# Batch 0 of an attention-and-experts kernel: normalising after the values product, and low key parts made by GpSimd

## The chip, the cores and the metric

The kernel runs on one core of a Trainium2 chip. The metric is device time in microseconds (us) of one execution. The profile is one profiled execution of the same program; its times are us from the start of its span unless marked ns.

## The reference

Attention over 4 batches of 8 heads, 576 positions, 64 columns a head, with a mask in blocks of 64; its output goes through two feed-forward stages.

```python
scores = scale * np.matmul(q, k.transpose(0, 1, 3, 2))
scores = np.where(block_i >= block_j, scores, -1000000000.0)
attn = np.exp(scores - np.max(scores, axis=-1, keepdims=True))
attn = attn / (np.sum(attn, axis=-1, keepdims=True) + 1e-09)
x = np.matmul(attn, v)                      # -> (2304, 512) over batches and heads
h = np.maximum(np.maximum(x @ w1, x @ w2), x @ w3)
x = h @ w_out                               # first feed-forward stage, d_ff 768
for e in range(4):                          # second stage, 4 experts, d_ff 1024
    out += p[:, e:e + 1] * (np.maximum(x @ w1[e], 0.0) @ w2[e])
```

All of it is float32. The division by the sum of a row is the normalising that the change moves.

## The kernel before

The program has three parts in time: the attention of batch 0, with nothing of the first feed-forward stage to fill TensorE; the attention of batches 1 to 3, between whose steps the first feed-forward stage (`moe1`, line 505) of the batch before is laid; and the second feed-forward stage, which takes the rest of the span.

Heads go in pairs (pairs 0 to 3 are batch 0). `prep_pair` makes of a pair's raw keys and queries a rounded high part and a low part that is the rest: of the keys, ScalarE rounds (line 85; of pair 0 VectorE, line 87) and VectorE subtracts on 64 partitions (line 122); of the queries, ScalarE rounds (133) and VectorE makes the rest (135). For pair 0 this goes head by head, for the others both heads in one instruction. `scores` multiplies them (190, and 195 for the mask), VectorE takes the row minimum of the negated scores (208), ScalarE takes the exponential with the row sum beside it (215). A head has four tiles of probabilities, 128, 384, 512 and 256 columns wide; a fifth, `p4`, 576 wide, holds the last 64 rows of both heads of a pair and is made with the second.

`normalise`, which is put in `later` and called one step after the scores, adds 1e-9 to the sums (223), takes their reciprocals (224), and GpSimd multiplies each tile of probabilities by its reciprocals in place (226). `turn_probs` then transposes the probabilities on TensorE (264) into PSUM, and ScalarE and VectorE copy them out to `eh` (273 and 289). Batch 0's `values32` multiplies them by the values (310, 318, 322) and ScalarE copies the result to `xf` (327 to 334). `xf` has the channels of both heads on its 128 partitions and the 576 positions along its columns. `moe1_inputs` splits `xf` into a high and a low part (523 and 524) for the feed-forward stage. Probabilities, transposes and scores share four PSUM banks (`ps_x`, tag `x`); `eh` has one buffer.

Beside this, from the first microseconds on, the class `Convert` turns 26 pieces of feed-forward weights from the 64-bit form in which they come into high and low parts: for each piece two instructions on ScalarE and one more to round (429, 431, 85), two on GpSimd (436, 443) and three on VectorE (438, 439, 452). They are needed by `moe1` of batch 0.

The order of each engine's instructions is not the order of the program text: a planner simulates the engines with a cost model of its own and orders each engine's instructions by what it takes to be ready first, so an edit in one place can change the order in others. Each engine then works through its list in order. Batch 0's pairs are `g < 4` in `prep_pair`, its heads `g < H` (8) elsewhere.

Of the kernel before, what the change touches and what calls it, by code (L numbers as in the profile page):

```python
# [6 lines left out]
F32 = mybir.dt.float32  # L7
# [5 lines left out]
ALU = mybir.AluOpType  # L13
# [5 lines left out]
P = 128  # L19
# [5 lines left out]
def program(tc, q, k, v, w123, w_out, probs, e_w1, e_w2, out):  # L25
    nc = tc.nc

    B, H, D, S = q.shape[0], 2 * q.shape[1], q.shape[2] // 2, q.shape[4]
# [12 lines left out]
    def f(ap):  # L41
        return ap.bitcast(F32)
# [3 lines left out]
    ident = const.tile([P, P], F32, name="ident")  # L46
# [10 lines left out]
    arena = big.tile([P, KD * NT], F32, name="arena")  # L57
# [8 lines left out]
    ps_x = attn.enter_context(tc.tile_pool(name="ps_x", bufs=4, space=PSUM, side="right"))  # L66
# [12 lines left out]
    lo, hi, both = slice(0, 64), slice(64, 128), slice(0, P)  # L79
# [25 lines left out]
    def prep_pair(g):  # L105


        raw, vraw = pairs[g]["raw"], pairs[g]["vraw"]
        if g < NPAIR and g % 2:

            spare = mp.tile([P, 2 * QW + 2 * S], F32R, name="spare", tag="hh")
            q1, q2 = spare[:, 0:QW], spare[:, QW:2 * QW]
            kk = spare[:, 2 * QW:].rearrange("x (h s) -> x h s", h=2)
        else:
            q1, q2 = (ap_.tile([P, QW], F32R, name=x, tag=x, bufs=1)[:] for x in ("q1", "q2"))
            kk = ap_.tile([P, 2, S], F32R, name="kk", tag="kk", bufs=1)[:]
        for x in (q1, q2):
            nc.gpsimd.memset(x[:, QT + 64:QT + 128].bitcast(U32), 0)

        def keys(hs):  # L120
            (rounded if g else lambda _, to, x: rounded(nc.vector, to, x))(nc.scalar, kk[:, hs], raw[:, 1, hs])
            nc.vector.tensor_tensor(kk[hi, hs], raw[hi, 1, hs], f(kk[hi, hs]), op=ALU.subtract)

        def queries(hs):
            x = raw[:, 0, hs]
            parts = []
            for to in (q1, q2):
                main = to[:, 0:QT].rearrange("x (h s) -> x h s", h=2)[:, hs]
                tail = to[:, QT:QW].rearrange("x (t s) -> x t s", s=64)[:, 0:3:2][:, hs]
                parts.append((main, tail))  # L130
            srcs = (x[:, :, 0:S - 64], x[:, :, S - 64:S])
            for high, src in zip(parts[0], srcs):
                nc.scalar.activation(high, src, ACTF.Copy, scale=-scale)  # L133
            for high, low, src in zip(*parts, srcs):
                nc.vector.scalar_tensor_tensor(low, src, -scale, f(high), op0=ALU.mult, op1=ALU.subtract)

        if g == 0:
            for h in range(2):
                keys(slice(h, h + 1))
                queries(slice(h, h + 1))  # L140
            yield
        else:
            keys(slice(0, 2))
            yield
            queries(slice(0, 2))
        pairs[g].update(q1=q1, q2=q2, kk=kk)
        if g < NPAIR:
            return
        vs = ap_.tile([P, 2, 5, P], F32R, name="vs", tag="vs", bufs=2)
        vh = vs[:, :, :, 0:64]  # L150
        src = vraw.rearrange("p j h d -> p h j d")
        rounded(nc.gpsimd, vh, src)
        nc.gpsimd.tensor_tensor(vs[:, :, :, 64:128], src, f(vh), op=ALU.subtract)
        pairs[g]["vs"] = vs
# [8 lines left out]
    def scores(g, grp):  # L163
        pair, h = pairs[g // 2], g % 2
        if grp == 0:
            heads[g] = dict(
                p=[None] * 4,
                mn=ap_.tile([P, 5], F32, name="mn", tag="mn", bufs=3),
                sm=ap_.tile([P, 5, 2], F32, name="sm", tag="sm", bufs=3),
            )  # L170
        mn, sm, pt = heads[g]["mn"], heads[g]["sm"][:, :, 0], heads[g]["p"]
        masked = g < 2 * H
        c0 = 3 * grp
        sets = []
        for tag, cols, plan in GROUPS[1][h] if grp else GROUPS[0]:
            st = (ps_x if tag == "x" else ps_c).tile([P, cols], F32, name="st", tag=tag)
            sets.append((st, plan))
            for i, o, w in plan:

                if i == 4:  # L180
                    todo = [(QT + 64 * x, x) for x in range(2)]
                else:
                    todo = [(h * QT // 2 + P * i, h)]
                c = 0
                while c < w:
                    n = min(w - c, 512 - (o + c) % 512)
                    terms = [(part, q0, x) for q0, x in todo for part in ("q1", "q2")]
                    ends = masked and i < 4 and c + n == w
                    for m, (part, q0, x) in enumerate(terms):
                        nc.tensor.matmul(  # L190
                            out=st[:, o + c:o + c + n], lhsT=pair[part][:, q0:q0 + P],
                            rhs=pair["kk"][:, x, c:c + n], start=m == 0, stop=m == len(terms) - 1 and not ends,
                        )
                    if ends:
                        nc.tensor.matmul(
                            out=st[:, o + w - 64:o + w], lhsT=corner, rhs=corner[:, 0:64], start=False, stop=True
                        )
                    c += n
        c = c0
        done = []  # L200
        for st, plan in sets:
            for i, o, w in plan:
                if i < 4 and not masked:
                    nc.vector.memset(st[lo, o + w - 64:o + w], 1e30)
            mine = [(c + n, *x) for n, x in enumerate(plan)]
            c += len(plan)
            for col, i, o, w in mine:
                nc.vector.tensor_reduce(mn[:, col:col + 1], st[:, o:o + w], axis=AX.X, op=ALU.min)  # L208
            for col, i, o, w in mine:
                x = ap_.tile([P, w], F32, name=f"p{i}", tag=f"p{i}", bufs=2 if i == 4 else 3)  # L210
                if i == 4:
                    pair["p4"] = x
                else:
                    pt[i] = x
                nc.scalar.activation(  # L215
                    x, st[:, o:o + w], ACTF.Exp, bias=mn[:, col:col + 1], scale=-1.0,
                    accum_out=sm[:, col:col + 1],
                )
                done.append((col, x))

        def normalise():
            cs = slice(c0, c)
            nc.vector.tensor_scalar(sm[:, cs], sm[:, cs], 1e-9, None, op0=ALU.add)  # L223
            nc.vector.reciprocal(sm[:, cs], sm[:, cs])
            for col, x in done:
                nc.gpsimd.tensor_scalar(x, x, sm[:, col:col + 1], 1.0, op0=ALU.mult, op1=ALU.mult)  # L226

        later.append(normalise)


# [70 lines left out]
    def values32(g, part):  # L301


        pair, hd, h = pairs[g // 2], heads[g], g % 2
        eh, vraw = pair["eh"], pair["vraw"]
        own = lo if h == 0 else hi
        both_v = [vraw[:, j].rearrange("p h d -> p (h d)") for j in range(5)]
        if part == 0:
            hd["pv"] = [ps_v.tile([P, 512], F32, name=f"pv{i}", tag="v") for i in range(2)]
            nc.tensor.matmul(  # L310
                out=hd["pv"][0][:, 0:P], lhsT=both_v[0], rhs=eh[:, ZERO + 4 * h], start=True, stop=True
            )
        pv = hd["pv"][1]

        for j in ((0, 1), (2, 3))[part]:
            q0 = P * (max(1, j) - 1)
            n = 3 - q0 // P + h
            nc.tensor.matmul(
                out=pv[:, q0:q0 + n * P], lhsT=both_v[j], rhs=row(eh, j, h, n), start=j == 0, stop=h == 0 and j == 3
            )  # L320
        if part and h:
            nc.tensor.matmul(out=pv[:, 384:512], lhsT=both_v[4], rhs=eh[:, LAST], start=False, stop=True)
        if part == 0 and h == 0:
            pairs[g // 2]["xf"] = mp.tile([P, S], F32, name="xf", tag="xf", bufs=4)
        xf = pairs[g // 2]["xf"]
        if part == 0:
            nc.scalar.copy(xf[own, 0:P], hd["pv"][0][own, 0:P])
            return
        if h == 0:
            nc.scalar.copy(xf[lo, P:512], pv[lo, 0:384])  # L330
        else:
            nc.scalar.copy(xf[hi, P:512], pv[hi, 0:384])
            nc.scalar.copy(xf[lo, 512:S], pv[lo, 384:448])
            nc.scalar.copy(xf[hi, 512:S], pv[hi, 448:512])
        del heads[g]

    def values(g, part):
# [294 lines left out]
    rt = ExitStack()  # L632
# [576 lines left out]
    for e in range(E):  # L1209
        for g in range(NG):  # L1210
            begins, ends = e == 0 and g == 0, e == E - 1 and g == NG - 1
            wo = []
            hs = [[], []]
# [129 lines left out]
```

## Time and profile before

| | |
|---|---|
| median of 3 runs | 1255.24 us (1250.58, 1255.24, 2066.23) |
| the profiled execution's own time | 1249.91 us, of which span 1248.1 us |
| TensorE matmul busy | 1211.2 us, 97% of the span |
| VectorE (DVE) busy | 929.7 us, 74% |
| ScalarE (ACT) busy | 517.8 us, 41% |
| GpSimd (POOL) busy | 357.1 us, 29% |
| granted TensorE clock, mean of the span | 0.996 |

Busy shares are means over stages with different limits. The change touches batch 0 alone, so what it is worth has to be read from the first stretch of the span, and from how that stretch hands over to the next.

### The profile page before, as it was taken

Reading aid. Unit: us, or ns where it says so; the run is one execution under the profiler, and the core shown is the slowest. Engines: PE = TensorE matmul, PEld = TensorE weight load, DVE = VectorE, ACT = ScalarE, POOL = GpSimd, SP = SyncE. Lnnn points to the kernel's source line nnn. Section 1 sums busy time; section 2 is a strip of 40 time slices with the busy share of each in tenths; the row PEclk is TensorE's granted clock in tenths of the full one; section 3 lists DMA queues with packets and bytes.
Section 4 is the critical chain, followed back from the end, with each engine's and each line's share of the span. In section 5 each row is a group of like instructions: output and inputs, shape, how many; then the busy total and the mean of one; then the engine's idle time right before and its main releaser. Section 6 shows DMA issues by size and latency. Waiting matters only on the chain.

```text
span 1248.1 us, 19730 instructions
## 1 busy us (share of the span) xinstructions
PE 1211.2 (97%) x7417; PEld 1157.8 (93%) x7417; DVE 929.7 (74%) x1716; ACT 517.8 (41%) x1076; POOL 357.1 (29%) x444
## 2 busy tenths in 40 slices
PE   7879998999999999999999999999999999999998
PEld 5669997999999999989999998999999999999998
DVE  7978988666565634377888896758787888686896
ACT  7977767544544421233444441233232223322222
POOL 3957786454344212243333341000000000000000
PEclk9999999999999999999999999999999999999999
DMA  8745574554533488478887864778888887776754
GB/s 304 248 164 197 170 265 161 172 153 155 183 102 119 120 287 304 150 303 332 312 311 296 310 247 162 287 274 316 300 306 311 315 314 281 253 258 228 253 210 170
DMA packets 82644, 299.69 MB, mean 240 GB/s; under 512 B 8748, under 2 KB 18036, under 8 KB 69492
## 3 DMA queue, kind: packets, MB, share of 16 engines
q1 hardware_dynamic: 82548, 298.42, 67.3%
q8 instruction: 59, 0.97, 0.3%
q14 instruction: 37, 0.30, 0.1%
HBM read 215.26 MB, written 83.14 MB: 239 GB/s over the span
## 4 chain that ended last, share of the span: by engine, by line
PE 74%; DVE 10%; DMA 5%; POOL 4%; ACT 3%; issue 3%; SPq 0%; DVEq 0%; ACTq 0%; POOLq 0%
PE m L858 24%; PE m L505 19%; PE o L1017 17%; PE st L190 3%; PE pv L359 2%; PE o L940 2%; PE o L943 2%; PE o L944 2%; DMA t<-in_e_w 2%; PE m L1017 2%; POOL p L226 2%; PE tt L264 2%; DVE mn L208 2%; DMA part<-in_e_w 1%; POOL arena L443 1%
## 5 line engine op out<-in xcount | busy, mean ns | idle before, releaser
L505 PE MATMUL m<-xh,wt 128*128 128x288 f32 x1120 | 238.4, 298 | 0.7 <-ACT mt L541 0.4
L858 PE MATMUL m<-t,w 128*128 128x384 f32 x1152 | 228.5, 336 | 0.0
L1017 PE MATMUL o<-hx,w 128*128 128x384 f32 x1176 | 225.7, 337 | 0.0
L1017 PEld LDWEIGHTS o<-hx,w 128*128 128x128 f32 x1176 | 207.8, 188 | 0.1
L858 PEld LDWEIGHTS m<-t,w 128*128 128x128 f32 x1152 | 203.4, 188 | 2.5 <-DVE tmp L878 0.4
L505 PEld LDWEIGHTS m<-xh,wt 128*128 128x128 f32 x1120 | 183.7, 188 | 1.6 <-DVE mt L543 0.8
L858 PE MATMUL m<-b,w 128*128 128x384 f32 x864 | 175.7, 337 | 2.0 <-ACT tmp L883 2.0
L505 PE MATMUL m<-xl,wt 128*128 128x288 f32 x560 | 165.3, 295 | 0.0
L858 PEld LDWEIGHTS m<-b,w 128*128 128x128 f32 x864 | 153.2, 188 | 5.1 <-ACT tmp L883 2.3
L226 POOL TENSOR_SCALAR p<-p,sm 128x128 f32<-128x128 f32 (+1 forms) x144 | 98.7, 702 | 52.1 <-DVE sm L223 17.0
L505 PEld LDWEIGHTS m<-xl,wt 128*128 128x128 f32 x560 | 105.3, 188 | 0.3
L878 DVE TENSOR_TENSOR tmp<-m,tmp 128x384 f32<-128x384 f32 x144 | 77.9, 550 | 19.4 <-PE m L858 19.2
L505 PE MATMUL m<-hh,wo 128*128 128x288 f32 x384 | 81.3, 299 | 2.9 <-ACT arena L554 1.3
L215 ACT ACTIVATE p<-st,mn 128x128 f32<-128x128 f32 (+3 forms) x144 | 78.5, 555 | 8.2 <-DVE mn L208 6.3
L988 ACT CAST hx<-hq 128x768 fp32r<-128x768 f32 x49 | 40.6, 837 | 99.0 <-PE o L1017 75.9
L190 PE MATMUL st<-kk,q 128*128 128x128 f32 (+4 forms) x336 | 71.2, 340 | 8.7 <-ACT q L133 5.5
L940 PE MATMUL o<-w,hh 128*128 128x512 f32 x192 | 74.7, 391 | 0.9 <-ACT hh L918 0.6
L813 POOL TENSOR_TENSOR w<-part,w 128x512 fp32r<-128x512 f32 x32 | 49.2, 1557 | 91.3 <-ACT w L811 61.2
L943 PE MATMUL o<-w,hh 128*128 128x512 f32 x192 | 74.7, 390 | 0.0
L944 PE MATMUL o<-w,hl 128*128 128x512 f32 x192 | 74.1, 390 | 0.0
L543 DVE TENSOR_TENSOR mt<-m,mt 128x288 f32<-128x288 f32 x96 | 43.2, 452 | 40.3 <-PE m L505 39.9
L264 PE MATMUL tt<-ident,p 128*128 128x128 f32 x400 | 61.0, 278 | 9.8 <-POOL p L226 5.4
(169 smaller groups left out, 2173.8 us busy)
## 6 DMA issues: line engine op xcount, KB each, us to landing
w<-kb SPq DMA_DIRECT2D x55, 1024.0 KB, 6.1
w<-ka SPq DMA_DIRECT2D x30, 1792.0 KB, 7.9
ka<-w SPq DMA_DIRECT2D x16, 1792.0 KB, 6.7
wt<-held SPq DMA_DIRECT2D x54, 512.0 KB, 4.1
kb<-part SPq DMA_DIRECT2D x16, 1024.0 KB, 7.0
kb<-w SPq DMA_DIRECT2D x16, 768.0 KB, 4.7
arena<-in_w SPq DMA_DIRECT2D x18, 512.0 KB, 4.0
wo<-held SPq DMA_DIRECT2D x12, 768.0 KB, 4.5
```

The source lines that it names most:

```text
L190: nc.tensor.matmul(out=st[:, o + c:o + c + n], lhsT=pair[part][:, q0:q0 + P], rhs=pair["kk"][:, x, c:c + n], start=m == 0, stop=m == len(t ...
L215: nc.scalar.activation(x, st[:, o:o + w], ACTF.Exp, bias=mn[:, col:col + 1], scale=-1.0, accum_out=sm[:, col:col + 1],)
L226: nc.gpsimd.tensor_scalar(x, x, sm[:, col:col + 1], 1.0, op0=ALU.mult, op1=ALU.mult)
L264: nc.tensor.transpose(tt[:, c:c + P], pt[i][:, k0:k0 + P], ident)
L505: nc.tensor.matmul(out=out_, lhsT=w, rhs=x, start=m == 0, stop=m == n - 1)
L813: eng.tensor_tensor(w[:, a:b, 1], raw[:, a:b], f(w[:, a:b, 0]), op=ALU.subtract)
L858: ins = nc.tensor.matmul(out=m, lhsT=a, rhs=b, start=start and n == 0, stop=stop and n == 3 * KH - 1, skip_group_check=True,)
L878: nc.vector.tensor_tensor(t, x, y, op=ALU.add)
L940: ins = nc.tensor.matmul(out=o, lhsT=hh[:, ts], rhs=wh, start=i == 0, stop=False)
L943: nc.tensor.matmul(out=o, lhsT=hh[:, ts], rhs=wl, start=False, stop=False)
L944: nc.tensor.matmul(out=o, lhsT=hl[:, ts], rhs=wh, start=False, stop=i == G - 1)
L1017: nc.tensor.matmul(out=o, lhsT=a, rhs=b, start=start and m == 0, stop=stop and m == 2, skip_group_check=True,)
```

## The change

In batch 0 the four tiles of a head's probabilities are no longer multiplied by the reciprocals of their row sums; the fifth tile, `p4`, still is. Instead GpSimd copies the reciprocals, each repeated over 64 columns, to `rb`, a place in an idle part of `arena` (two places, taken by turns of the pairs): per head one copy of three columns of reciprocals and one of a single column. After the pair's values product, TensorE transposes the four 128x128 blocks of `rb` into a PSUM tile `rt` of the four shared banks, which makes them a tile of reciprocals by channel and position, and VectorE multiplies the first 512 columns of `xf` by it. And for batch 0's pairs GpSimd takes over the subtraction that makes the low part of the keys, but for that of the very first head.

```diff
         def keys(hs):
-            nc.vector.tensor_tensor(kk[hi, hs], raw[hi, 1, hs], f(kk[hi, hs]), op=ALU.subtract)
+            (nc.gpsimd if g < 4 and hs != slice(0, 1) else nc.vector).tensor_tensor(
+                kk[hi, hs], raw[hi, 1, hs], f(kk[hi, hs]), op=ALU.subtract
+            )
...
             nc.vector.reciprocal(sm[:, cs], sm[:, cs])
+            if g < H:
+
+                if grp == 0 and h == 0:
+                    o = (2 + 4 * (g // 2 % 2)) * P
+                    pair["rb"] = arena[:, o:o + 4 * P].rearrange("p (i h c) -> p i h c", i=4, h=2)
+                rb = pair["rb"][:, 0:3, h] if grp == 0 else pair["rb"][:, 3:4, h]
+                rs = sm[:, c0:c] if grp == 0 else sm[:, c - 1:c]
+                nc.gpsimd.tensor_copy(rb, rs.unsqueeze(2).to_broadcast([P, c - c0 if grp == 0 else 1, 64]))
             for col, x in done:
+                if g < H and x is not pair.get("p4"):
+                    continue
                 nc.gpsimd.tensor_scalar(x, x, sm[:, col:col + 1], 1.0, op0=ALU.mult, op1=ALU.mult)
...
             nc.scalar.copy(xf[hi, 512:S], pv[hi, 448:512])
+
+            rt = ps_x.tile([P, 512], F32, name="rt", tag="x")
+            for n, i in enumerate((0, 2, 3, 1)):
+                nc.tensor.transpose(
+                    rt[:, P * i:P * (i + 1)], pair["rb"][:, n].rearrange("p h c -> p (h c)"), ident
+                )
+            nc.vector.tensor_tensor(xf[:, 0:512], rt, xf[:, 0:512], op=ALU.mult)
         del heads[g]
```

## Rows read from the trace of the kernel before

**Rows 1.** Busy us (and instructions) of each engine by stretch, granted clock, DMA share, GB/s.

```profile
10.00:20.00 10.00, 7.74 (x38) 6.60 (x36) 7.33 (x19) 9.72 (x24) 3.93 (x9) 0.86 1.03 414
...
30.00:40.00 10.00, 8.70 (x55) 6.80 (x53) 9.69 (x17) 9.90 (x26) 9.75 (x13) 1.00 0.79 263
40.00:50.00 10.00, 8.31 (x40) 6.06 (x39) 9.81 (x18) 9.13 (x25) 8.46 (x11) 0.83 0.54 186
...
60.00:70.00 10.00, 8.29 (x50) 6.32 (x51) 5.83 (x16) 7.76 (x20) 8.13 (x12) 1.00 0.51 174
...
100.00:120.00 20.00, 19.32 (x142) 18.15 (x142) 17.73 (x35) 13.02 (x29) 19.34 (x24) 1.00 0.58 187
```

**Rows 2.** The chain of work, 0 to 92 us: start, us, what.

```profile
by line: POOL p L226 11.9%; DVE mn L208 8.9%; issue 8.3%; PE pv L318 7.1%; POOL arena L443 6.7%; PE st L190 6.2%; ACT p L215 5.6%; DMA arena<-in_q 5.4%; DVE spare L122 4.0%; PE tt L264 3.3%; PE m L505 3.0%; DVE q L135 2.3%; DVE xl L524 2.2%
...
11.41 1.35 DVE spare L122
...
19.96 1.50 DVE kk L122
...
31.03 2.33 DVE spare L122
...
44.55 2.29 POOL p L226 x4
...
60.67 2.05 POOL p L226 x4
...
78.97 2.36 POOL p L226 x2
...
82.03 4.49 PE pv L318 x8
...
89.17 2.21 PE m L505 x16
```

**Rows 3.** GpSimd's groups by shape, 0 to 90 us: busy us, mean ns, idle before.

```profile
L226 POOL TENSOR_SCALAR p<-p,sm 128x384 f32<-128x384 f32 x10 | 7.7, 765 | 0.0
L226 POOL TENSOR_SCALAR p<-p,sm 128x512 f32<-128x512 f32 x10 | 7.4, 738 | 0.0
L226 POOL TENSOR_SCALAR p<-p,sm 128x256 f32<-128x256 f32 x10 | 7.2, 725 | 0.0
...
L226 POOL TENSOR_SCALAR p<-p,sm 128x128 f32<-128x128 f32 x10 | 4.3, 432 | 5.3 <-ACT p L215 2.0 <-ACT wo L85 1.9 <-DVE sm L224 0.9
```

**Rows 4.** Line 226 alone, 76 to 90 us: ns min/median/max, first and last start.

```profile
L226 POOL TENSOR_SCALAR p<-p,sm x9: 367/690/1651, 78.6 to 86.6; 128x128 f32<-128x128 f32 x2, 128x384 f32<-128x384 f32 x2, 128x512 f32<-128x512 f32 x2, 128x256 f32<-128x256 f32 x2
```

**Rows 5.** Who waited for whom, 0 to 92 us: us in total, times, longest.

```profile
PEld tt L264 <- POOL p L226: 7.3, 4, 4.6
...
PEld st L190 <- DVE eh L289: 1.9, 2, 1.5
```

**Rows 6.** Single lines over the whole span: ns min/median/max, first and last start.

```profile
L122 DVE TENSOR_TENSOR kk<-arena,kk x9: 755/1355/1885, 4.6 to 343.9; 64x1152 fp32r<-64x1152 f32 x7, 64x576 fp32r<-64x576 f32 x2
...
L122 DVE TENSOR_TENSOR spare<-raw,spare x2: 1355/1842/2329, 11.4 to 31.0; 64x1152 fp32r<-64x1152 f32 x2
...
L153 POOL TENSOR_TENSOR vs<-vraw,vs x12: 1553/1572/2034, 39.5 to 381.2; 128x640 fp32r<-128x640 f32 x12
...
L546 POOL TENSOR_TENSOR hl<-mt,hh x48: 793/807/1792, 110.0 to 501.8; 128x288 fp32r<-128x288 f32 x48
...
L118 POOL MEMSET q<- x28: 147/152/163, 1.0 to 369.1; 128x64 uint32 x28
```

**Rows 7.** VectorE's groups by shape, 0 to 90 us.

```profile
L292 DVE TENSOR_TENSOR eh<-tt,eh 128x512 fp32r<-128x512 f32 x2 | 1.3, 687 | 3.5 <-ACT eh L291 3.5
```

**Rows 8.** Instructions in order of time, TensorE 24 to 26 us, VectorE 14 to 17 us.

```profile
24.75 1.07 PE L264 MATMUL tt<-ident,p 128*128 128x128 f32 x8
...
15.99 0.27 DVE L135 SCALAR_TENSOR_TENSOR spare<-raw,spare 128x128 fp32r<-128x128 f32 x1
```

**Rows 9.** TensorE alone by stretch: busy us, granted clock, DMA share, GB/s.

```profile
82.00:84.00 2.00, 2.00 (x4) 0.50 0.47 177
```

## The prediction, made before the result was known

> **What bounds the kernel now.** I read the table of busy time by stretch first. There the reader is to see two regimes. From 100 us on TensorE is busy 19.32 of 20 us; in batch 0's stage, from 30 to 50 us, it is busy 8.3 to 8.7 of 10, while VectorE shows 9.69 and 9.81, ScalarE 9.90 and 9.13 and GpSimd 9.75 and 8.46 [rows 1]. So batch 0 is bound by three engines at once, none of them TensorE, and what follows by TensorE. Then the chain of work up to 92 us: batch 0 hands over at 89.17, where line 505 begins [rows 2]. A microsecond taken out ahead of that point can be worth a microsecond at the end, since what follows is mostly a full TensorE; after it, the change alters nothing but the planner's order.
>
> The chain shows which engine ends last and where. VectorE's low keys (line 122) stand in it with 1.35 us at 11.41, 1.50 at 19.96 and 2.33 at 31.03; GpSimd's normalising (226) with 11.9% of 92 us, 10.9 us [rows 2]. Both are what the change takes away, so the naive reading is a gain of 5.2 and 10.9 us. Two things cut it. The first is whose normalising it is: GpSimd has treated ten tiles of each shape by 90 us, so ten heads [rows 3], and the nine instructions that start between 78.6 and 86.6 us are those of the last two of them, heads 8 and 9, which are batch 1's and keep theirs [rows 4]. The piece of 2.36 us at 78.97 [rows 2] therefore stays, and with it the one wait of 4.6 us that is most of the 7.3 us that TensorE's transposes wait for line 226 [rows 5]. The second is what is late next, which is taken stretch by stretch below.
>
> **What it removes and adds, engine by engine.** *GpSimd*: a head's four tiles cost 0.432 + 0.765 + 0.738 + 0.725 = 2.66 us [rows 3], eight heads 21.3 us, gone. Added are three low keys of 1152 columns and one of 576. GpSimd has no such row; its two-input float32 rows are 1.572 us for 640 columns and 0.807 for 288 [rows 6], that is 2.17 ns a column and 0.18 us to start with, hence about 2.68 and 1.43 us, 9.5 us in all. By VectorE's own 1.355 as the lower end it is 4.7, by the slowest of the 640-column rows (2.034 us, 3.18 ns a column) 12.8; I take 9.5, as the two rows do the same operation. Added too are sixteen copies of repeated reciprocals. No row shows one: the 64-column clearing of 0.152 us [rows 6] is a lower end for each, the 384-column product at 0.765 [rows 3] an upper. I take 0.45 us for three columns and 0.25 for one, near the 128-column row (0.432), 5.6 us in all, between 2.4 and 12.2. GpSimd is so left 21.3 - 9.5 - 5.6 = 6.2 us less to do.
>
> *VectorE*: four instructions of line 122 go, 0.755 + 1.355 + 1.50 + 2.33 = 5.9 us [rows 2 and 6]. Added are four products of `rt` with `xf`, each of 128x512 with one input in PSUM, as the subtraction of line 292, 0.687 us [rows 7]: 2.7 us. Net 3.2 us less.
>
> *TensorE*: sixteen more transposes. Eight of them take 1.07 us at the full clock [rows 8], so 0.13 each and 2.1 us together. They lie in a stage in which TensorE is idle 1.3 to 2.3 of every 10 us [rows 1]; cost nothing while that cover lasts, 2.1 us without it. *ScalarE* loses and gains no instruction.
>
> **The new waits.** A low key on GpSimd waits for ScalarE's rounding; behind it on GpSimd are the clearing for the next pair's queries, `p4`'s normalising and weight pieces (436, 443). Its reader, the scores, wants the low queries as well, and these come later from VectorE: for pair 1 they end at 16.26 us [rows 8], while the low keys, begun at 11.41, would end near 14.1, and at the upper price of 3.66 us at 15.1. So the slower engine isn't waited for; VectorE, on which line 135 no longer stands behind line 122, can be done earlier. The product with `rt` waits for the last copy of `xf` by ScalarE and for the transposes; behind it on VectorE stand the next head's row minima, for which the exponentials wait. For the last pair it lies between `xf` and the split of line 523, some 0.7 us, but only the fourth of `moe1`'s input blocks needs it, so I take that as hidden by the first three; uncovered it is 0.7 us. The copies to `rb` are done a whole values product before their use: nothing.
>
> **What is late next, stretch by stretch.** 10 to 30 us: 2.85 us of line 122 leave the chain [rows 2]; head 0's transposes no longer wait for line 226, in a stretch in which TensorE has 2.3 us idle of the first 10. But ScalarE is busy 9.72 of those 10 [rows 1]: I take half, 1.5 us. 30 to 40 us: 2.33 leave, ScalarE is busy 9.90 [rows 1], so it is next, and only the weight pieces laid there can give way: 1. 40 to 60 us: the four tiles at 44.55 (2.29 us) leave the chain [rows 2], VectorE is busy 9.81 in the first half [rows 1]: 1. 60 to 70 us: 2.05 us leave [rows 2], and here VectorE (5.83) and ScalarE (7.76) have room [rows 1]: 2, the whole. 70 to 89 us: nothing, as the wait there belongs to head 8. Sum 5.5 us. From it go half of the products with `rt`, 1.4 us, for those that fall into the full stretches of VectorE, and 0.6 us for weight pieces that come later when the holes in which they lay are closed. That leaves **3.5 us**.
>
> [...] Pair 1's low key took 1.355 us on VectorE with GpSimd idle, pair 3's, at 31.03, with GpSimd at work, 2.329 [rows 2, 6]. [...]
>
> **The rivals.**
> 1. *Given back.* The holes close, but the weight pieces that filled them move behind 89 us, where GpSimd is as full (19.34 of 20) as TensorE [rows 1], or the planner keeps TensorE's order, so that the transposes stand where they stood and the edit does nothing for them. For it: three engines at over 90% from 30 to 50 us. Against it: GpSimd and VectorE have 9.4 us less to do in sum. No change, 1250 to 1251 us.
> 2. *Contention.* Each of GpSimd's four low keys stretches VectorE's work beside it as GpSimd's work stretched line 122, by 0.97 us: 3.5 - 3.9, nothing left of the gain, 1251 us. Against it: the low keys on GpSimd are 9.5 us in place of 21.3.
> 3. *The bank.* Slower. `rt` takes one of the four banks that scores and transposes share, and holds it from its first transpose to the end of VectorE's product, which waits for ScalarE's copies. Scores already waited 1.9 us, at most 1.5 at once, for a bank to be copied out by line 289 [rows 5]. If the planner lays the transposes early, every pair pays such a wait: 4 x 1.5 = 6 us, with the gain gone, 1256 to 1257 us. It decides when `rt` is held longer than about 1.5 us; transposes and product alone are 0.54 + 0.69 = 1.2, so it hangs on the order.
> 4. *More.* The planner, with head 7 done earlier, also lays its values product ahead of head 8's transposes. [...]
>
> **How the numbers follow.** The sum is made against the profiled execution, 1249.9 us, whose span is 1248.1; two of the timed runs, 1250.6 and 1255.2, lie 0.7 and 5.3 above it, the third, 2066, is far off and not counted. The listed median, 1255.2, is the upper of the two. I count from the middle one of the three close times, 1250.6: less 3.5 gives 1247. Chances: forecast 0.45 (its own range 1244 to 1250), given back 0.25, contention 0.05, bank 0.10, more 0.15. The range reaches from just under the case of more to just over that of the bank, 1239 to 1257, which also takes in the 5 us by which two runs of one kernel differ. About 2%, 25 us, is what a measurement of this kernel can tell from no change. All the line 122 and 226 pieces of the chain together are 16 us, and no rival has a price near 25, so both ends get little: faster 0.02, within 0.96, slower 0.02.
>
> **What would show it.** Right: line 505 begins some 3 to 6 us before 89.17; VectorE has no line 122 in batch 0 but one; GpSimd shows 2.7 us for it, and scores of pair 1 begin before 16.2; line 226 is left with `p4` ahead of head 8; the wait of transposes for line 226 is still one of about 4.6 us. The bank would show as scores or transposes that wait for the product with `rt`; a gain given back, as more idle time of TensorE between the start of line 505 and 200 us. Wrong it would be if the chain there turns to GpSimd's low keys, if the copies to `rb` cost far over 0.45 us, or if the stretch up to 505 is shorter and the end is not.

## The result, and the profile after

The change makes the kernel slower: the ratio of its runs to runs of the kernel before is 1.0055, 95% interval 1.0042 to 1.0068 (median 1260.46 us beside 1254.97), some 7 us where 3.5 us less were forecast. One run of each kernel, 2066 and 6333 us, lies far out and is left out of the ratio. The profiled execution took 1258.38 us, its span 1256.6 against 1248.1.

Busy time by stretch, the changed kernel; columns as in [rows 1]:

```profile
10.00:20.00 10.00, 8.09 (x36) 6.62 (x37) 8.38 (x18) 8.85 (x25) 4.19 (x7) 0.90 1.00 388
20.00:30.00 10.00, 6.65 (x39) 5.04 (x38) 8.46 (x14) 9.19 (x25) 6.87 (x7) 0.93 0.44 160
30.00:40.00 10.00, 9.87 (x50) 7.50 (x50) 7.18 (x12) 7.03 (x17) 5.87 (x8) 0.83 0.65 220
40.00:50.00 10.00, 7.01 (x43) 5.06 (x42) 9.93 (x23) 8.70 (x25) 4.71 (x6) 1.00 0.84 303
...
100.00:120.00 20.00, 19.31 (x146) 18.48 (x146) 16.89 (x40) 14.98 (x37) 15.14 (x20) 1.00 0.56 191
```

One stretch of the kernel before that [rows 1] lacks:

```profile
20.00:30.00 10.00, 9.31 (x55) 6.63 (x54) 9.97 (x23) 8.91 (x26) 6.07 (x9) 0.97 0.64 241
```

GpSimd has what was meant: from 30 to 50 us it is busy 5.87 and 4.71 in place of 9.75 and 8.46. But TensorE, the engine that should have gained, is down from 9.31 to 6.65 from 20 to 30 us, and from 8.31 to 7.01 from 40 to 50; from 30 to 40 it is up from 8.70 to 9.87, at a granted clock of 0.83 in place of 1.00.

The changed kernel's line 524 is line 505 of before (the line 524 of before that is shown further down is another, on VectorE). Its first and last start, and below it those of the product with `wo`, whose last is the end of the first feed-forward stage:

```profile
L524 PE MATMUL m<-xh,wt x1120: 288/295/401, 93.4 to 505.7; 128*128 128x288 f32 x187
...
L524 PE MATMUL m<-hh,wo x384: 288/295/406, 189.6 to 525.3; 128*128 128x288 f32 x192
```

Before, these were 89.0 and 518.9. So in the profiled executions 4.4 us are lost by the handover, 6.4 by the end of that stage, and 8.5 over the span. The values products of batch 0's last two heads (6 and 7), before and after, show that more than 4.4 us had been lost on the way:

```profile
70.66 2.19 PE L318 MATMUL pv<-eh,vraw 128*128 128x384 f32 x8
81.87 4.66 PE L318 MATMUL pv<-eh,vraw 128*128 128x512 f32 x8
```
```profile
78.64 2.19 PE L330 MATMUL pv<-eh,vraw 128*128 128x384 f32 x8
87.86 3.06 PE L330 MATMUL pv<-eh,vraw 128*128 128x512 f32 x8 [1.98 <-ACT eh L301]
```

That of head 6 begins 8.0 us later than before; 3.6 of these are won back by the handover.

Who waited for whom up to 96 us, and the wait of the transposes of reciprocals (line 350), from the groups by shape, in the changed kernel:

```profile
PE rt L350 <- DVE eh L301: 4.4, 3, 3.0
PE st L192 <- DVE eh L301: 2.7, 1, 2.7
```
```profile
L350 PE MATMUL rt<-ident,arena 128*128 128x128 f32 x16 | 2.5, 278 | 4.4 <-DVE eh L301 4.4
```

The waits of transposes for line 226 [rows 5] are gone from the list, also the one of 4.6 us that was forecast to stay. In their place TensorE stands 4.4 us in front of `rt`, with all the scores and transposes queued behind it, until VectorE's copy (301) has emptied one of the four shared banks. The longest of these waits, and what VectorE did ahead of it, in order of time:

```profile
12.21 2.64 POOL L122 TENSOR_TENSOR spare<-raw,spare 64x1152 fp32r<-64x1152 f32 x1 [3.59 <-ACT spare L85]
...
12.85 2.03 DVE L225 TENSOR_SCALAR sm<-sm 128x3 f32<-128x3 f32 x1 [1.20 <-ACT p L217]
...
26.15 2.68 POOL L122 TENSOR_TENSOR kk<-arena,kk 64x1152 fp32r<-64x1152 f32 x1
26.39 3.00 DVE L458 SCALAR_TENSOR_TENSOR arena<-arena 128x512 uint32<-128x512 uint32 x1
...
29.31 0.68 DVE L301 COPY eh<-tt 128x512 f32<-128x512 f32 x1
...
30.13 0.63 PE L350 MATMUL rt<-ident,arena 128*128 128x128 f32 x4 [3.02 <-DVE eh L301]
...
42.26 0.68 DVE L353 TENSOR_TENSOR xf<-rt,xf 128x512 f32<-128x512 f32 x1
```

Two things are to be seen. Line 225 on three columns takes 2.03 us and line 458 takes 3.00, and both end just after GpSimd's line 122 does (12.21 + 2.64 = 14.85, against 14.88; 26.15 + 2.68 = 28.83, against 29.39). I read this as VectorE standing still for the rest of GpSimd's instruction and then doing its own work. The same line 458 takes 0.68 at 41.06, and line 225 on three columns 0.15 at 40.99, with GpSimd idle. And `rt`, written from 30.13 on, is read at 42.26: one of four banks is gone for 42.94 - 30.13 = 12.8 us. The other three pairs hold it 12.5, 8.7 and 7.1 us.

The stand reaches TensorE by another way too. The scores of pair 1 begin at 15.42 us (16.24 before), but the low queries (line 137), which VectorE makes behind line 225, are late:

```profile
17.50 0.33 PE L192 MATMUL st<-spare 128*128 128x128 f32 x1 [1.78 <-DVE spare L137]
```

### The profile page after: what moved, and what is told of

The parts are those of the page before. It is cut to its first block, busy times and chain, and to the rows that moved or that the text cites. A ratio compares the mean times of both kernels' runs of the same rounds, so it can differ in the third digit from the quotient of the medians.

```text
span 1256.6 us, 19753 instructions
## 1 busy us (share of the span) xinstructions
PE 1217.6 (97%) x7433; PEld 1163.1 (93%) x7433; DVE 931.4 (74%) x1716; ACT 517.9 (41%) x1076; POOL 347.9 (28%) x432
## 4 chain that ended last, share of the span: by engine, by line
PE 67%; DVE 13%; DMA 9%; ACT 5%; issue 3%; POOL 3%; SPq 0%; DVEq 0%; ACTq 0%; POOLq 0%
PE m L877 20%; PE m L524 19%; PE o L1036 16%; DMA t<-in_e_w 5%; PE st L192 3%; DMA part<-in_e_w 2%; PE tt L276 2%; PE pv L378 2%; PE m L1036 2%; ACT p L217 2%; DVE w L832 1%; POOL p L238 1%; DVE mn L210 1%; DVE tmp L897 1%; DVE hl L938 1%
## 5 line engine op out<-in xcount | busy, mean ns | idle before, releaser
L238 POOL TENSOR_SCALAR p<-p,sm 128x128 f32<-128x128 f32 (+4 forms) x112 | 75.9, 694 | 48.3 <-DVE sm L226 23.5
L210 DVE TENSOR_REDUCE mn<-st 128x1 f32<-128x128 f32 (+3 forms) x144 | 66.4, 504 | 3.5 <-PE st L197 3.1
```

## The experiments

Two theories: the *port* (VectorE held up by GpSimd's low keys; the name is only a label, as the traces show that VectorE stands, up to 3.00 - 0.68 = 2.32 us at once in the changed kernel, and not what holds it) and the *bank* (`rt` in a bank that TensorE's queue waits for). The third, the *planner*, says that any edit shifts the order, and neither cost is real. Ratios are to runs of the kernel before on the same chip; "begins" is the first matmul of the feed-forward stage (89.0 before, 93.4 in the changed kernel), "ends" its last start of the product with `wo` (518.9 and 525.3). These two are of one profiled execution each, and the granted clock is in them: from 0 to 90 us its mean was 0.94 before and in the changed kernel, 0.91 to 0.98 in the others, and 0.01 of it over 90 us is, by my estimate, 0.9 us of work at the full clock (0.01 x 90).

| kernel | low keys | `rt` | ratio, 95% interval | begins | ends |
|---|---|---|---|---|---|
| the change | GpSimd, whole | shared bank | 1.0055, 1.0042 to 1.0068 | 93.4 | 525.3 |
| late_only | VectorE | shared bank | 1.0040, 1.0024 to 1.0056 | 92.7 | 525.5 |
| keys_pieces | GpSimd, pieces | shared bank | 1.0011, 0.9999 to 1.0023 | 88.5 | 518.8 |
| rt_later | GpSimd, whole | shared bank, one step later | 1.0035, 1.0022 to 1.0049 | 89.1 | 520.1 |
| rt_in_pv | GpSimd, whole | idle bank | 1.0018, 1.0006 to 1.0031 | 90.9 | 520.0 |
| late_rt_pv | VectorE | idle bank | 0.9989, 0.9980 to 0.9998 | 88.0 | 517.1 |
| rt_pv_pieces | GpSimd, pieces | idle bank | 0.9984, 0.9972 to 0.9996 | 85.7 | 514.7 |
| keys_twice | VectorE, and idle copies on GpSimd | idle bank | 1.0041, 1.0028 to 1.0053 | 93.2 | 523.3 |
| no_rt | GpSimd, whole | none | 0.9995, 0.9983 to 1.0006 | 86.8 | 518.2 |
| keys_only | GpSimd, whole | normalising as before | 0.9995, 0.9985 to 1.0006 | 89.3 | 518.8 |
| keys_only_pieces | GpSimd, pieces | normalising as before | 0.9979, 0.9970 to 0.9988 | 84.0 | 516.0 |

**late_only.** Late normalising without the move of the keys.

```diff
-            (nc.gpsimd if g < 4 and hs != slice(0, 1) else nc.vector).tensor_tensor(...)
+            nc.vector.tensor_tensor(kk[hi, hs], raw[hi, 1, hs], f(kk[hi, hs]), op=ALU.subtract)
```

> Late normalising alone: all low keys by VectorE again. [...] Theory of the bank (the tile of reciprocals holds one of four PSUM banks for 7 to 13 us in every pair): still 1257 to 1260 us, line 524 begins after 92 us. [...]

1.0040, a median of 1258.58 us, with the start at 92.7: the bank's numbers. Were VectorE's stands beside the low keys the whole cost, it would be back near the kernel before. The groups by shape show TensorE waiting in front of `rt` longer still:

```profile
L348 PE MATMUL rt<-ident,arena 128*128 128x128 f32 x16 | 2.9, 315 | 7.1 <-DVE sm L223 3.9 <-DVE eh L299 3.3
```

Of these, 3.9 us are put down to line 223, which came last by the semaphores but writes nothing that `rt` needs. For the wait that ended at 64.24 the order of time shows VectorE's copy out of a bank (299) ending at 64.13, 0.14 us before TensorE starts at 64.27 (in the changed kernel it was 29.99 to 30.13), so I read these as the bank too.

**keys_only.** The kernel before with nothing but the move of the low keys to GpSimd.

> Low keys by GpSimd alone, normalising as before. Port: slower than the kernel before by 4 to 8 us, 1255 to 1259 us, and VectorE instructions of 2 to 3 us beside GpSimd's line 122. Bank: no tile of reciprocals, so as the kernel before or 1 to 3 us under it, 1247 to 1252 us.

0.9995: no change. Not the 4 to 8 us of the port, nor a gain. The long VectorE instructions that the port expected are there all the same: 2.03 us at 12.26 and 2.08 at 25.00, each beside a line 122 of GpSimd. So the stands cost nothing that the time shows; that a gain of the move cancels them is a reading that keys_only_pieces fits.

**keys_pieces.** The whole change, GpSimd's subtraction cut into four.

```diff
+            if g < 4 and hs != slice(0, 1):
+                for x in range(hs.start, hs.stop):
+                    for c in range(0, S, S // 2):
+                        cs = slice(c, c + S // 2)
+                        nc.gpsimd.tensor_tensor(kk[hi, x, cs], raw[hi, 1, x, cs], f(kk[hi, x, cs]), op=ALU.subtract)
...
```

> The whole change, with each low key on GpSimd cut into pieces of 288 columns, by the rows 0.8 us each. Port: no VectorE instruction stands still for more than about 0.8 us beside them, where it was up to 2.3; 2 to 4 us come back, 1255 to 1257 us. Bank: nothing comes back, 1258 to 1261 us.

1.0011: 5.5 us came back, more than the 2 to 4 of the port, though GpSimd's own time for the low keys rose from 9.4 to 13.0 us. VectorE's longest stand beside them fell from 2.32 to 0.63 us, and the wait in front of `rt` fell with it:

```profile
L354 PE MATMUL rt<-ident,arena 128*128 128x128 f32 x16 | 2.9, 315 | 2.1 <-DVE eh L305 1.2 <-ACT p L221 0.6 <-POOL arena L466 0.4
```

`rt` itself holds its bank as long as ever (14.5 us in the first pair, 25.32 to 39.80). So the two costs meet: a bank comes free when VectorE has copied it out, and a VectorE that stands still for GpSimd keeps the bank. From here on the two are taken as partners.

**rt_in_pv.** The whole change, `rt` in the PSUM bank of the second head's first values product, of which only 128 columns were ever used.

```diff
-            rt = ps_x.tile([P, 512], F32, name="rt", tag="x")
-            for n, i in enumerate((0, 2, 3, 1)):
+            rt = hd["pv"][0]
+            for n, i in ((1, 2), (2, 3), (3, 1), (0, 0)):
```

> The whole change, with the transposed reciprocals in the bank of the second head's first values product, which is idle by then, so that none of the four shared banks is taken. Bank: 4 to 7 us come back, 1252 to 1255 us, and line 524 begins some 4 us earlier than 93.4. Port: nothing comes back, 1257 to 1260 us.

1.0018: 4.6 us come back (0.37% of 1252), at the low end of the 4 to 7 of the bank; the start, at 90.9 us, is 2.5 us earlier and not 4.

**late_rt_pv.** Both edits above, late_only and rt_in_pv: the cleanest measure of the bank, since between the programs of late_only and this only the place of `rt` differs.

> Late normalising alone, with the transposed reciprocals in the idle bank of the values product. Bank: late_only's 3.3 us at the handover come back and more, since its TensorE waited 7.2 us for banks in front of the transposes: the feed-forward stage begins at 85 to 88.5 us, 1247 to 1251 us. If late normalising costs by something other than the bank: 1255 us or more.

0.9989 against 1.0040: 0.51%, 6.4 us, for the place of one PSUM tile. Late normalising by itself is a gain, but of 1.4 us (0.3 to 2.5 by the interval).

**no_rt.** The whole change without transposes and product; it leaves batch 0's first 512 positions undivided.

```diff
-            rt = ps_x.tile([P, 512], F32, name="rt", tag="x")
-            ...
-            nc.vector.tensor_tensor(xf[:, 0:512], rt, xf[:, 0:512], op=ALU.mult)
```

> The whole change without the transposes of the reciprocals and without VectorE's product with them: batch 0's first 512 positions stay undivided by their sums. After batch 0 its order on TensorE is the one of the kernel before. Theory of the bank (TensorE stands in front of the transposes of the reciprocals until one of four banks is free, 4.4 us in the changed kernel): the 4.4 us and half of the products come back, line 524's counterpart begins at 87 to 89.5 us, 1249 to 1253 us. Theory of the port: the low keys are still on GpSimd and still hold VectorE up, begins after 91 us, 1255 to 1259 us.

It begins at 86.8, just ahead of the 87 to 89.5 of the bank, and has 0.9995, as the bank said. Even with the step left out, 2.2 us at the handover become 0.7 at the end of the stage.

**rt_later.** Transposes and product are put in `later`, which runs them behind the next step of the program.

```diff
+            def put_in():
+                rt = ps_x.tile([P, 512], F32, name="rt", tag="x")
+                ...
+            put_in() if g == H - 1 else later.append(put_in)
```

> The whole change, with transposes and product put off by one step of the program, but for the last pair. Bank: if the planner then lays the transposes later, the bank is held for fewer us and TensorE's wait in front of them is under 3 us; 2 to 4 us come back, 1254 to 1257 us. If it lays them as early as before, nothing: 1258 to 1261 us. Port: nothing comes back either way.

1.0035: 2.5 us come back, inside the 2 to 4, but the two intervals overlap. TensorE no longer waits in front of `rt`, but the bank is still held 5.9 to 10.4 us, and the wait has moved to the next transposes of probabilities, which need the bank that the product with `rt` must free; from the list of waits up to 96 us:

```profile
PE st L192 <- DVE eh L301: 3.8, 4, 1.4
PE tt L276 <- DVE xf L354: 2.3, 2, 1.5
```

**rt_pv_pieces.** Both cures: keys_pieces and rt_in_pv.

> Both cures together: low keys on GpSimd in pieces of 288 columns, transposed reciprocals in the idle bank. Bank and port each with its share: begins at 85 to 88 us, 1246 to 1251 us. Bank alone: as rt_in_pv, begins near 91 us, 1253 to 1256 us. Planner alone: neither follows.

0.9984, beside 1.0011 and 1.0018 with one cure alone, and it begins at 85.7: each cure has its share.

**keys_twice.** late_rt_pv, with needless work on GpSimd.

```diff
+            if 0 < g < 4:
+                spot = arena[hi, 1280:2304].rearrange("p (h s) -> p h s", h=2)
+                nc.gpsimd.tensor_tensor(spot, raw[hi, 1, :, 0:512], f(kk[hi, :, 0:512]), op=ALU.subtract)
```

> late_rt_pv (ratio 0.9989; VectorE makes the low keys) with three needless GpSimd subtractions of 1024 columns on 64 partitions, from the raw and the low keys of pairs 1 to 3 into idle memory: the suspected cost of the port alone, with nothing taken from VectorE. Port: three stands of VectorE of 1 to 2.4 us each, 3 to 6 us slower than late_rt_pv, 1254 to 1257 us. If GpSimd's subtractions cost only what waits for their result: as late_rt_pv, 1250 to 1252 us.

1.0041 against late_rt_pv's 0.9989: 0.52%, 6.5 us for three instructions whose result nobody reads, over the upper end. In order of time, one of them beside VectorE:

```profile
27.18 2.43 POOL L125 TENSOR_TENSOR arena<-arena,kk 64x1024 f32<-64x1024 f32 x1
```
```profile
27.30 2.33 DVE L226 TENSOR_SCALAR sm<-sm 128x3 f32<-128x3 f32 x1
29.55 0.68 DVE L459 SCALAR_TENSOR_TENSOR arena<-arena 128x512 uint32<-128x512 uint32 x1
```

27.18 + 2.43 = 29.61, and VectorE's three columns end at 29.63. So such instructions on GpSimd cost by themselves, with no low key moved. How much of the 6.5 us is VectorE's stands isn't parted: GpSimd also has 8.0 us more to do, and TensorE's order and clock differ too (0.91 up to 90 us, 0.94 in late_rt_pv).

**keys_only_pieces.** The kernel before, low keys on GpSimd in pieces of 288 columns, normalising untouched.

> Low keys alone by GpSimd as in keys_only (ratio 0.9995 to the kernel before), but in pieces of 288 columns. Port: VectorE's instructions stand still for no more than the rest of a piece, some 0.8 us instead of up to 2; 1 to 3 us come back, 1248 to 1251 us. If pieces helped in keys_pieces only through the banks that VectorE's late copies kept, nothing: 1251 to 1253 us.

0.9979, the lowest ratio here, and 0.16%, 2.0 us, under keys_only, which differs by the cut alone. VectorE's stands beside the low keys fell from 4.3 us in sum to 2.3, the longest from 1.88 to 0.62. But the transposes' wait for GpSimd's normalising fell too, here keys_only and then this run, up to 96 us, and no run parts the two:

```profile
PE tt L266 <- POOL p L228: 7.1, 4, 4.3
```
```profile
PE tt L270 <- POOL p L232: 3.3, 3, 1.3
```

It begins 5.0 us before the kernel before, but ends the stage only 2.9 before it, and of this the ratio shows 2.6. Where it went, by stretch from 160 to 200 us, where TensorE was busy 36.64 us before, at a granted clock of 1.00 where it is 0.96 here:

```profile
160.00:200.00 40.00, 34.27 (x233) 32.17 (x232) 35.90 (x82) 26.80 (x65) 32.22 (x40) 0.96 0.65 219
```

## Why the prediction failed, point by point

*What bounds batch 0.* Right: three engines together, and a handover that decides most of it. The pieces of batch 0's lines 122 and 226 left the chain, and the copies to `rb` cost 0.23 to 0.34 us alone, inside their bounds.

*The wait that was to stay.* Wrong, and in the change's favour. "70 to 89 us: nothing, as the wait there belongs to head 8", but in the changed kernel head 8's transposes stand behind the last values product, at 90.98 us, and the product takes 3.06 us in place of 4.66, at a granted clock of 1.00 from 86 to 92 us where it was 0.50 from 82 to 84 [rows 9]. That is the order that the rival *more* had named. It came with the loss and not with a gain: the 3.6 us won back in this stretch hide that 8.0 had been lost ahead of it. The lower end of the range, 1239 us, rests on the time of *more*, which no run shows: the product fell by 1.6 us in this profile, at a median of 1260.46 us, and the lowest time of any run is 1245.67 us, in rt_pv_pieces.

*The price of a low key on GpSimd.* 2.68 us was forecast; lines of the changed kernel by source:

```profile
L122 POOL TENSOR_TENSOR spare<-raw,spare x2: 2642/2644/2647, 12.2 to 36.2; 64x1152 fp32r<-64x1152 f32 x2
...
L353 DVE TENSOR_TENSOR xf<-rt,xf x4: 677/682/694, 42.3 to 91.7; 128x512 f32<-128x512 f32 x4
```

Right, as is the product with `rt` (0.687 forecast).

*The bank: the step that failed first.* Its mechanism and its place were named, with a chance of 0.10, at 1.5 us a pair and a deciding point of 1.5 us of holding, and the sum put it at nothing. `rt` was held 7.1 to 12.8 us. The mistake was to count the step's own 1.2 us and to leave the order open. The order could have been read off: the transposes need only `rb`, which the prediction itself had ready "a whole values product before their use", and a planner that lays first what is ready first lays them there, ahead of the scores in a queue that works in order. What is ready early and read late holds its place for the whole time between. Moved to an idle bank, the same change gained 0.37% (whole keys) and 0.51% (keys on VectorE).

*The contention: mis-sized.* The price of 0.97 us each came from line 122 at 31.03, where GpSimd had only 1.1 us still to do (30.55 + 1.59 - 31.03). Taking each VectorE instruction beside GpSimd's line 122 less the time that its like takes alone, the changed kernel stands 6.2 us in sum, not 3.9: 2.32 (line 458), 1.88 (225), 1.66 (137 at 37.05) and smaller ones. The prediction weighed against it that 9.5 us of low keys came in place of 21.3 us of other GpSimd work. The stands beside that work were about as many us in sum (4.6 to 6.7, by the median or the shortest of their like), but none was over 1.0 us, as most of those instructions (29 of 36 up to 78 us) took under 0.75. So what changed is the length of the single stand, and the runs in pieces fit that: with more GpSimd time and shorter instructions the time fell. The row was there to be read, in the trace of before:

```profile
39.45 1.68 POOL L153 TENSOR_TENSOR vs<-vraw,vs 128x640 fp32r<-128x640 f32 x1
39.64 2.10 DVE L524 TENSOR_TENSOR xl<-xf,xh 128x576 fp32r<-128x576 f32 x1
```

39.45 + 1.68 = 41.13, plus the 0.75 us that line 524 needs alone, is 41.88, close to its end at 41.74.

*That the two meet.* The prediction listed bank and contention as rivals, each with its own chance. In the changed kernel both came, and of the 3.02 us in front of the first `rt` 2.32 were a VectorE stand, handed on through a bank. That one makes the other dearer over the whole time isn't shown: the idle bank was worth 0.37% with whole keys on GpSimd, 0.51% with the keys on VectorE and 0.27% with pieces, too close for their intervals.

*The gain.* 3.5 us were forecast; the change with both costs cured gives 0.16%, 2.0 us, and without the keys (late_rt_pv) 1.4 us. So the sign was right and the size, by the middle values, 1.5 to 2 us too large. The place was wrong: the sum had its 5.5 us won by 70 us, but in late_rt_pv the values product of head 6, at 70.66 before, begins at 72.06, and only the last one, at 79.89 in place of 81.87, is earlier. Among all the runs that product is earlier only in rt_pv_pieces (68.08) and keys_only_pieces (68.99). TensorE's order ahead of it differs from run to run, so these starts are a sign and not a measure. That a gain at the handover is partly given back was seen in no_rt and keys_only_pieces.

*What the handover doesn't hold.* Of the 8.5 us of the span 2.0 come between handover and end of the stage, and 2.1 behind it. By my estimate TensorE's granted clock accounts for most of both. TensorE alone in the changed kernel by stretch, columns as in [rows 9]:

```profile
200.00:204.00 4.00, 2.97 (x23) 1.00 0.27 98
204.00:208.00 4.00, 3.16 (x13) 0.73 0.60 133
208.00:212.00 4.00, 4.00 (x29) 0.85 0.91 359
760.00:764.00 4.00, 2.67 (x16) 1.00 0.41 130
764.00:768.00 4.00, 2.45 (x7) 0.70 0.50 185
768.00:772.00 4.00, 4.00 (x18) 0.87 0.00 0
```

Before, it was 1.00 in all six. What is missing is (0.27 + 0.15) x 4 = 1.7 us at the full clock in the first drop, and as much in the second ((0.30 + 0.13) x 4); ahead of each lies a stretch with idle time, TensorE busy 2.97 and 2.67 of 4 us. The same 1.7 us stand in no_rt (0.94 and 0.63 from 196 to 204 us), which gives back 1.5 us in that stage, and in late_only (0.64 and 0.93 from 220 to 228), which loses 2.9. It isn't so everywhere: rt_in_pv has 0.83 from 190 to 200 us and loses nothing in the stage.

*What stays open.* Why the clock falls in one order of work and not in another is not shown: the kernel before has as much idle time from 208 to 216 us (busy 3.24 and 2.39 of 4) and stays at 1.00. Nor is the planner ruled out as a part of any single ratio, as no run keeps TensorE's order and changes one cost. Counted from the end of the program back, 6628 of the changed kernel's 7433 TensorE matmul records stand in the order of before, 7026 in keys_pieces, 5349 in late_rt_pv and 4040 in rt_in_pv. Against the planner alone stands that in every run but keys_only the ratio went the way that the bank or the port had said. The profiled spans are single ones: runs of the kernel before differ by 6 us (1250.4 to 1256.7 in 29 runs).

## What to carry to other kernels

When a step takes a slot of a pool that the main path also draws from, price the time from the moment its inputs are ready to the moment its reader runs, because that is how long a planner that goes by readiness can hold the slot; here a bank that lay idle at that time was worth 0.3 to 0.5%. When work is moved to GpSimd beside a busy VectorE, look at GpSimd's longest single instruction, not at the sum, and cut it: here four pieces of 0.8 us did the work of one of 2.64 and made the move of the keys a gain, of 0.21%. Two prices that are rivals in a forecast can both come due; where they meet at one resource, as here a bank that VectorE empties, the forecast needs the case of both.

## What the runs showed of the hardware

A VectorE instruction on three columns that took 0.15 us with GpSimd idle (line 225 of the changed kernel at 40.99) took 2.03 us there at 12.85, beside a two-input GpSimd instruction of 2.64, and 2.33 us in keys_twice at 27.30, beside one of 2.43. These two ended 0.03 and 0.02 us after GpSimd's instruction: in these rows the whole rest of it is waited for. VectorE instructions with two inputs of their own took longer as well: line 458 of the changed kernel 3.00 us beside line 122, where it took 0.68 with GpSimd idle, and line 524 of the kernel before 2.10 us beside line 153, where its median is 0.755. What holds VectorE in these rows is not shown.
